# Two attention blocks on one Trainium2 core: the memory block's feature map is computed as a guarded quadratic on VectorE and GpSimd, two chunks are normalised in one pass, four squared tiles a unit, and the first chain of operations is shortened

## The chip, the cores and the metric

The kernel runs on one core of a Trainium2 chip. A core has TensorE (PE, matrix multiplications into PSUM), ScalarE (ACT, activation functions), VectorE (DVE) and GpSimd (POOL) for elementwise work, and SyncE (SP), which here only issues transfers. Each engine works through a queue of its own in order; semaphores tie the queues together. PSUM has eight banks of 128 x 512 f32.

The metric is the time of one execution in microseconds on the device, as the median of several runs. A profile is one execution, taken by itself; it shows every instruction with start and duration.

## The reference

There are two independent blocks, whose outputs stand side by side. S = 2048 rows, D = 1024, H = 32 heads of 32 columns.

```python
def _A_ref(x, wqkv, wo):                        # plain attention, no mask
    q, k, v = split(x @ wqkv)                   # per head [2048, 32]
    p = softmax(q @ k.T * Dh ** -0.5)
    return (p @ v) @ wo

def _B_ref(x, wq, wk, wv, wo, beta):            # four segments of L = 512 rows, causal inside a segment
    phi = lambda t: where(t > 0, t + 1.0, exp(t))
    M, z = 0, 0
    for s in range(4):
        qs, ks, vs = segment s of x @ wq, x @ wk, x @ wv
        a_dot = softmax(qs @ ks.T * Dh ** -0.5 + causal mask) @ vs
        pq = phi(qs)
        a_mem = (pq @ M) / (pq @ z + 1e-6)
        o = g * a_mem + (1 - g) * a_dot         # g = sigmoid(beta), one number a head
        pk = phi(ks)
        M, z = M + pk.T @ vs, z + sum(pk)
    return concat(o) @ wo
```

All entries of x, wqkv and wo are normal numbers times 0.05; B's weights are smaller by another factor of 32 (`D ** -0.5`). Inputs are bf16.

## The kernel before

**Units.** Four heads (128 partitions) are worked on together: a group g = 0..7. A's unit (g, c) is a chunk c = 0..7 of 256 queries against all 2048 keys. B's unit (s, j) is a pair of groups j, j+1 of one segment. B's 16 units are strewn among A's 64. The first four units of A are cut into parts, so that work can begin before all of x is there.

**Sets.** A unit consists of sets: eight in A, five in B, 592 in all. A set is four score tiles, one for each head, of 128 keys x 512 columns in four PSUM banks. TensorE fills them with eight (or twelve) small matmuls, tiled by rows (L1194, `plan_set`). ScalarE then takes the exponential, two banks (1024 columns) at a time (L1270, `plan_exp`), without a maximum subtracted. Three pairs of banks rotate for this, and two further banks serve everything else on TensorE. The products with V (L1361) and the row sums (L1368, `round`) are matmuls tiled by columns, and so are all projections (L822, `mm4`). Between two score sets TensorE therefore does column work: sums of older sets and projection "jobs" for later units.

**Squared tiles.** In some sets of an A unit the first head's tile doesn't go to ScalarE: VectorE computes Y = a x + b from PSUM (L1231), GpSimd squares it (L1234, `plan_square`). The constant part that this approximation of the exponential leaves out is added back when a chunk is normalised (`corr`, `cu`). `SQUARES` lists the sets for each g: five of eight for g = 0 and 1, four for g = 2 to 6, three for g = 7.

**The guard.** Both the missing maximum and the squares are valid for small scores only. For every projection the squared norms of q and k are bounded (`guard_cols`, `guard_dg`, `guard_more`, `guard_end`; squares by `square` and `square_dve`), and a flag is set. ScalarE's program exists twice; at 24 places it loads a flag and branches. In the guarded copy every exponential has a bias, and squared tiles are redone by an exponential (`alt`). With the present data the plain copy runs.

**Norms.** When a chunk's sums are complete (`norm`, `recip_rows`), VectorE copies them from PSUM to a buffer T2 while adding the correction (L1427), transposes the row sums (L1429), takes reciprocals (L1442), transposes back (L1444); GpSimd multiplies (L1493, L1488). B's norms begin with a transpose and a scaled copy from PSUM (L1431, L1433) and end with two operations on GpSimd (L1507, L1508). T2 has a ring of three buffers (`T_RING`) for these, and one more for B's memory reads (`job_mem`), which normalise 512 columns in the same manner.

**The feature map** (`job_phi`). For B's group (s, j) ScalarE takes exp of k, of q, or of both (L1906, 512 or 1024 columns, from SBUF), VectorE takes the minimum with 1 (L1908) and adds max(x, 0) (L1912). The result PKQ goes to the memory read and, by a transposing transfer, to the update of M (`job_M`).

**The order.** All operations are written down once with keys. A planner (`Prog.schedule`) then simulates the engines with costs given for each operation and writes the queues: exponentials stay in program order, TensorE chooses between score sets, sums and jobs, jobs carry due times (`level`, `plan_jobs`, `NUDGE`), and a table `SHIFT` moves single keys of VectorE, GpSimd and ScalarE. The costs only set the order; on the chip semaphores alone hold the engines.

**The start** (`plan_prologue`). x is fetched in six transposing transfers on SyncE's queue (L1546, `X_PIECES`; `turn`), with weights between them (L1517, L1523). The first K and Q of group 0 are projected (`quarter`), copied (L1776 on VectorE, L1778 on ScalarE), squared (L1817), reduced (L1614), and the bias of the first guarded exponentials (L1257) is computed (L1624, L1691, L1697, L1700).

## Time and profile before

| | us |
|---|---|
| median of 3 runs | 1057.02 (1055.73 to 1057.83) |
| profiled execution, its own time | 1059.17 |
| its span (first to last instruction) | 1057.3 |
| granted TensorE clock | 0.997 of full speed |

The profile's page names instructions by line and engine. "Busy" is the time in which an engine has at least one instruction under way; for TensorE the ends are modelled, and matmuls overlap. A group's row reads: line, engine, operation, output <- inputs, shapes, count | busy us, mean ns of one | idle time of the engine just before them, and what ended most of it. A timeline's row reads: start, length, engine, line, operation, count, and in brackets idle time before it; several equal instructions in a row are merged. Rows of the page that stand for the rest, in us:

| engine | busy | share of the span | instructions |
|---|---|---|---|
| TensorE | 1023.4 | 97% | 25438 |
| ScalarE | 1016.9 | 96% | 1224 |
| VectorE | 701.6 | 66% | 1562 |
| GpSimd | 585.9 | 55% | 677 |

### The profile page before, as it was taken

The page shows a single profiled execution, that of the slowest core. Times are in us where ns is not written, and L with a number is a line of the kernel's source. Part 1 is how long each engine was busy: PE and PEld are TensorE (multiplying, and loading weights), DVE is VectorE, ACT ScalarE, POOL GpSimd, SP SyncE. Part 2 cuts the span into 40 slices and gives each one's busy share as a digit, 9 for nine tenths or more (in the row PEclk, how much of TensorE's full clock was granted, in tenths as well). Part 3 has the DMA queues.
Part 4 walks back from the last instruction along what each step waited for, and adds up shares of the span by engine and source line. Part 5 has one row for each costly group of instructions (what it writes and reads, how often), then busy time and mean ns, then how long its engine had stood idle before and what let it go on. Part 6 is the DMA issues. An engine that isn't in the chain of part 4 may idle for free.

```text
span 1057.3 us, 56117 instructions
## 1 busy us (share of the span) xinstructions
PE 1023.4 (97%) x25438; PEld 561.2 (53%) x25438; DVE 701.6 (66%) x1562; ACT 1016.9 (96%) x1224; POOL 585.9 (55%) x677
## 2 busy tenths in 40 slices
PE   8999999999999999999999999999999989999998
PEld 3555555655555555555555545565555545445554
DVE  2356866667566586767865598687755875874444
ACT  3999989999999999999999999999999999999997
POOL 2115467558654675756656487665644765653310
PEclk9999999999999999999999999999999999999999
DMA  9132352005313241032223330132113551021101
GB/s 189 34 90 58 69 126 46 10 21 120 83 48 92 64 103 25 11 82 66 58 57 95 96 69 19 25 93 54 50 28 91 161 174 27 23 78 54 56 23 62
DMA packets 171390, 72.17 MB, mean 68 GB/s; under 512 B 134800, under 2 KB 169360, under 8 KB 171152
## 3 DMA queue, kind: packets, MB, share of 16 engines
q1 hardware_dynamic: 168784, 67.79, 26.2%
q8 instruction: 200, 3.28, 1.4%
q10 hardware_dynamic: 2368, 0.79, 0.3%
q14 instruction: 38, 0.31, 0.1%
HBM read 45.29 MB, written 11.73 MB: 54 GB/s over the span
## 4 chain that ended last, share of the span: by engine, by line
PE 58%; ACT 34%; DVE 4%; issue 2%; SPq 1%; DMA 1%; ACTq 0%; DVEq 0%
ACT P L1270 33%; PE ps L822 28%; PE ps L1194 12%; PE ps L1361 9%; PE ps L1368 8%; PE ps L1862 1%; SPq L1546 1%; DVE Y L1231 1%; DMA xT_A<-in_A_x_dram 1%; ACT PKQ_B L1906 1%; DVE T L1431 0%; DVE KQ_B L1581 0%; PE ps L1637 0%; DVE OT_B L1933 0%; DVE T L1444 0%
## 5 line engine op out<-in xcount | busy, mean ns | idle before, releaser
L1270 ACT ACTIVATE P<-ps 128x1024 bf16<-128x1024 f32 (+1 forms) x1176 | 989.4, 1062 | 16.3 <-PE ps L1194 8.0
L1234 POOL TENSOR_TENSOR Pc<-Y 128x512 bf16<-128x512 f32 x238 | 249.6, 1050 | 266.3 <-PE ps L822 84.8
L1368 PE MATMUL ps<-P,onesb 128*32 128x256 bf16 (+1 forms) x4388 | 295.1, 271 | 0.6 <-issue 0.6
L1361 PE MATMUL ps<-P,V_A 128*32 128x256 bf16 x3620 | 252.1, 274 | 0.7 <-DVE cols L1691 0.2
L1231 DVE TENSOR_SCALAR Y<-ps 128x512 f32<-128x512 f32 x238 | 163.3, 686 | 104.5 <-PE ps L1194 95.5
L1194 PE MATMUL ps<-KQ_A 32*128 32x256 bf16 x4096 | 203.9, 273 | 11.6 <-ACT P L1270 7.3
L1194 PEld LDWEIGHTS ps<-KQ_A 32*128 32x128 bf16 x4096 | 61.7, 92 | 157.7 <-ACT P L1270 115.7
L822 PE MATMUL ps<-xT_A,W_A 128*32 128x512 bf16 (+1 forms) x2232 | 138.8, 363 | 3.0 <-DMA xT_A<-in_A_x_dram 2.5
L1368 PEld LDWEIGHTS ps<-P,onesb 128*32 128x32 bf16 x4388 | 128.4, 97 | 24.7 <-issue 11.4
L822 PE MATMUL ps<-xT_B,W_B 128*32 128x512 bf16 (+1 forms) x2264 | 139.2, 360 | 2.3 <-issue 0.6
L1361 PEld LDWEIGHTS ps<-P,V_A 128*32 128x32 bf16 x3620 | 107.4, 96 | 25.7 <-issue 10.6
L1368 PE MATMUL ps<-Pc,onesb 128*32 128x256 bf16 x476 | 119.3, 274 | 0.0
L1361 PE MATMUL ps<-Pc,V_A 128*32 128x256 bf16 x476 | 119.1, 274 | 0.1
L1293 POOL TENSOR_SCALAR_AFFINE_SELECT P<-P 128x768 bf16<-128x768 bf16 (+1 forms) x96 | 75.7, 794 | 48.3 <-ACT P L1270 46.2
L1595 POOL TENSOR_TENSOR sqA<-KQ_A 128x512 bf16<-128x512 bf16 x61 | 63.4, 1048 | 66.7 <-DVE KQ_A L1581 34.6
L1595 POOL TENSOR_TENSOR sqB<-KQ_B 128x512 bf16<-128x512 bf16 x64 | 67.8, 1061 | 19.9 <-DVE KQ_B L1581 15.1
L822 PEld LDWEIGHTS ps<-xT_B,W_B 128*32 128x32 bf16 x2264 | 52.8, 96 | 48.7 <-issue 19.9
L822 PEld LDWEIGHTS ps<-xT_A,W_A 128*32 128x32 bf16 x2232 | 51.8, 96 | 50.7 <-issue 16.9
L1444 DVE STREAM_TRANSPOSE T<-rc 128x256 f32<-128x256 f32 (+1 forms) x152 | 72.5, 481 | 2.7
L822 PE MATMUL ps<-Wv_B,xT_B 128*32 128x512 bf16 (+1 forms) x1128 | 70.7, 361 | 2.1 <-issue 1.3
L822 PE MATMUL ps<-Wo_B,OT_B 128*32 128x512 bf16 (+1 forms) x1128 | 69.0, 361 | 0.3 <-DVE T L1427 0.3
L1581 DVE CAST KQ_B<-ps 128x512 bf16<-128x512 f32 x64 | 43.9, 685 | 32.2 <-PE ps L822 31.5
(114 smaller groups left out, 1231.4 us busy)
## 6 DMA issues: line engine op xcount, KB each, us to landing
Wv_B<-in_B_wv_dram SPq DMA_DIRECT2D x32, 256.0 KB, 3.4
W_B<-in_B_wk_dram SPq DMA_DIRECT2D x32, 256.0 KB, 3.2
W_B<-in_B_wq_dram SPq DMA_DIRECT2D x32, 256.0 KB, 3.9
Wo_B<-in_B_wo_dram SPq DMA_DIRECT2D x32, 256.0 KB, 3.2
out_dram<-outsb SPq DMA_DIRECT2D x56, 128.0 KB, 1.8
W_A<-in_A_wqkv_dram SPq DMA_DIRECT2D x14, 256.0 KB, 3.9
ot_a_scratch<-OTst SPq DMA_DIRECT2D x51, 64.0 KB, 2.3
xT_A<-ot_a_scratch SPq DMA_DIRECT2D x6, 512.0 KB, 5.8
```

The source lines that it names most:

```text
L822: ins = e.matmul(out[r], w[:, r], x, start=start, stop=stop, tile_position=(0, 32 * t), skip_group_check=True)
L1194: ins = e.matmul(out, kap, qap, start=st, stop=True, tile_position=(32 * h, 0), skip_group_check=True)
L1231: o = self.dve(lambda e: e.tensor_scalar(Y[:, :], src, KAPPA * SCALE, BETA, ALU.mult, ALU.add), 512, key - 9.0, [self.bank[bank]], [rY], f ...
L1234: last.append(self.pool(lambda e: e.tensor_tensor(dst, Y[:, :], Y[:, :], ALU.mult), 512, key - BCK, [rY], [rP], rate=0.56))
L1270: a = self.act(guarded if early else lambda e: e.activation(dst, src, ACT.Exp, scale=SCALE), cols, key, rd, wr, fixed=EXP_FIXED + (0.095 i ...
L1293: self.pool(lambda e: e.affine_select(v, v, pattern=pat, compare_op=ALU.is_ge, fill=0.0, base=0, channel_multiplier=-1), 2 * nd * P, key + ...
L1361: ins = e.matmul(self.pb(obk, q0, q0 + nq, slice(32 * h, 32 * h + 32)), v, p, start=first, stop=last, tile_position=(0, 32 * h), skip_grou ...
L1368: ins = e.matmul(self.pb(obk, QC + q0, QC + q0 + nq, slice(32 * h, 32 * h + 32)), self.onesb[:, 0:32], p, start=False, stop=last, tile_pos ...
L1444: self.dve(lambda e: e.transpose(L2.rearrange("p (b r) -> p b r", r=32), bc), n, key, [rr], [rl], fixed=0.17)
L1546: return self.dma(lambda e: e.dma_start(dst, src, transpose=True), sem, key, reads, writes, issue=issue, lat=lat, gate=gate)
L1581: self.dve(lambda e: e.tensor_copy(dst, src()), 512, key, [self.at(b)], rdst, fixed=0.155)
L1595: self.pool(lambda e: e.tensor_tensor(sq[:, :], src, src, ALU.mult), 512, key, [rsrc], [rs], rate=0.56)
```

## The change

1. **Feature map.** `job_poly` computes min((a x + b)^2 + 1 - b^2, 1) with a = 0.6909, b = 0.7232 instead of min(exp(x), 1): VectorE writes U = a x + b (512 columns, f32), GpSimd squares U in place and then adds and takes the minimum into PKQ. U is a single buffer. `job_phi` keeps only the sum with max(x, 0). The work is placed about half an A unit ahead of the A unit that runs before the B unit ("host"); the projections of B's k and q are due before the host, too. The guard's limit for B becomes much smaller (`FREE_B`), and the guarded copy of ScalarE's program redoes the exponential (`redo`, `late` in `plan_exp`).
2. **Squares.** `LEVEL` replaces the list by g: four squared tiles in every unit of g = 0 to 6, three for g = 7. There are 226 squared tiles where there were 238.
3. **Norms.** Two successive chunks of A with squares share one transpose, one reciprocal and one transpose back; the copy from PSUM stays one a chunk. T2 has four buffers: two for these pairs, two that all other norms and the memory reads share.
4. **The start.** ScalarE squares Q straight from PSUM before it copies it; the norms' matmuls accumulate two halves, so that the reduction is over 256 columns; one operation of the first bias is left out. SyncE's queue waits after the fourth piece of x until that piece has landed; two later pieces and three weight transfers are behind this wait.
5. **Order.** The table `SHIFT` has new entries, so that the order of VectorE's, GpSimd's and ScalarE's queues differs in many places.

```diff
-T_RING = 3
-PHI_AT = 4.341
+PHI_AT, PHI_G, PHI_LEAD = 4.341, 0.0, 6.0
-FREE = 0.1
+FREE, FREE_B = 0.1, 0.5 * SCALE * 0.01
+QUAD = 0.6909020858999743, 0.7231874996921336
-SQUARES = ((1, 3, 4, 6, 7), (1, 3, 4, 6, 7), (1, 3, 4, 6), (1, 3, 5, 7), (1, 3, 5, 7), (1, 3, 5, 7), (1, 3, 5, 7), (1, 4, 6))
+SQUARES = ((1, 3, 4, 6, 7), (1, 3, 5, 7), (1, 4, 6))
+LEVEL = "1111111111111111" "1111111111111111" "1111111111111111" "1111111122222222"
+ALONE = ((6, 6), (6, 7))
...
-        if add is None:
-            i = self.nT % T_RING
-            self.nT += 1
-        else:
-            i = T_RING
-        T2, rc = self.T2[i], self.rc[i]
+        i = 2 + self.nT % 2
+        self.nT += 1
+        T2, rc = self.T2[:, i, :], self.rc[i - 1]
...
+        if cu is not None and (g, t["c"]) not in ALONE:
+            n = int(self.half is not None)
+            ok = self.T2[:, n, :].rearrange("p (a n) -> p a n", a=2)
+            self.dve(lambda e: e.tensor_tensor(ok, self.pb(obk).rearrange("p (a n) -> p a n", a=2),
+                                               cu[0].unsqueeze(2).to_broadcast([P, 2, QC]), ALU.add), 512, k - NORM_K, [ob, cu[1]],
+                     [self.r_T2[n]], fixed=0.155)
+            if not n:
+                self.half = t
+                return
+            both, rr = self.r_T2[:2], self.r_rc[0]
+            L2, rc = self.T2[:, 0:2, QC:512], self.rc[0][:, :].rearrange("p (a b) -> p a b", a=2)
+            self.dve(lambda e: e.transpose(L2, L2), 512, k, both, both, fixed=0.17)
+            self.dve(lambda e: e.reciprocal(rc, L2.rearrange("p a (b r) -> p a b r", r=32)[:, :, :, 0]), 128, k, both, [rr])
+            self.dve(lambda e: e.transpose(L2.rearrange("p a (b r) -> p a b r", r=32), rc.unsqueeze(3).to_broadcast([P, 2, 8, 32])), 512, k,
+                     [rr], both, fixed=0.17)
+            for i, x in enumerate((self.half, t)):
+                self.scaled(x, k, self.T2[:, i, 0:QC], self.T2[:, i, QC:512], [self.r_T2[i]])
+            self.half = None
+            return
...
+                o = self.turn(self.xT[:, lo:hi, 512 * h:512 * h + 512], xa[512 * h:512 * h + 512, P * lo:P * hi],
+                              self.sm_x[n], key, [], rs, issue, lat)
+                if n == 3:
+                    gate = o
+                if n >= 4:
+                    o.deps.add(gate)
+                    if n == 5:
+                        o.order.add(last)
+                last = o
...
+                    self.act(lambda e, x=direct[0], src=src: e.activation(x[:, :], src, ACT.Square), 512, key, [bk], [direct[1]])
                     self.act(lambda e, dst=dst, src=src: e.activation(dst, src, ACT.Copy), 512, key, [bk], [rd])
...
-                self.colrun = self.guard_cols(key, sq, bank=3)
-                self.guard_end(key, [self.colrun], 2, [BIAS_PART[0]], bank=4, urgent=True)
+                self.colrun = self.guard_cols(key, sq, bank=3, wide=QC)
+                self.guard_end(key, [self.colrun], 2, [BIAS_PART[0]], bank=4, urgent=True, raw_bias=True)
...
+    def job_poly(self, s, j, key, at):
+
+        holds(self.r_KQB[j], "KQ", s, j)
+        mark(self.r_PKQ[j % 2], "P", s, j)
+        PKQ, rp, ks = self.PKQ[j % 2], self.r_PKQ[j % 2], self.phi_of(s)
+        a, b = ks[0], ks[-1] + 1
+        made = []
+        U, rU = self.U, self.r_U
+        for k in ks:
+            x = PKQ[:, k, :]
+            self.dve(lambda e, k=k: e.tensor_scalar(U[:, :], self.KQB[:, j, k, :], QUAD[0], QUAD[1], ALU.mult, ALU.add), L / 2, key,
+                     [self.r_KQB[j][k]], [rU], fixed=0.16, port=True)
+            self.pool(lambda e: e.tensor_tensor(U[:, :], U[:, :], U[:, :], ALU.mult), L, key + PHI_G, [rU], [rU], rate=0.56)
+            made.append(self.pool(lambda e, x=x: e.tensor_scalar(x, U[:, :], 1.0 - QUAD[1] ** 2, 1.0, ALU.add, ALU.min), L, key + PHI_G,
+                                  [rU], [rp[k]], rate=1.0))
+        self.phi_redo[s, j] = dict(at=at, op=None, made=made, reads=[self.r_KQB[j][k] for k in ks], rp=rp[a:b], out=PKQ[:, a:b, :],
+                                   src=self.KQB[:, j, a:b, :], bc=2 + j // 2)
+
     def job_phi(self, s, j, key):
...
-        x = self.act(lambda e: e.activation(PKQ[:, a:b, :], src, ACT.Exp), n, key, rs, rp[a:b], fixed=0.19)
-        x.margin = MARGIN
-        self.dve(lambda e: e.tensor_scalar(PKQ[:, a:b, :], PKQ[:, a:b, :], 1.0, None, ALU.min), n / 4, key, rp[a:b], rp[a:b], fixed=0.16,
-                 port=True)
-        for k in range(a, b):
+        for k in self.phi_of(s):
...
-                d = min(SB[j - j % 2] - LEAD_B, SB[RXJ] - 1.0)
+                d = min(self.host[s, j - j % 2] - LEAD_B, SB[RXJ] - 1.0)
...
-                r = SB[j] - 4.0 - PHI_AT
+                at = self.host[s, j - j % 2]
+                self.item(at - PHI_LEAD + 0.01 * (j % 2), lambda key, s=s, j=j, at=at: self.job_poly(s, j, key, at))
+                r = max(at + 1.0, SB[j] - 4.0 - PHI_AT)
```

More of the change, by code (lines that the diff above doesn't have):

```diff
@@ L480, in ready_of @@
             for x in o.deps:
[L481 removed]
+                t = max(t, x.end + (SELF if x.eng == o.eng and x.sem is None else x.lat) + (job if x.eng in ("DVE", "POOL") else 0.0) +
                         (TO_POOL if o.eng == "POOL" and x.eng == "DVE" else 0.0) +
@@ L1041, in plan @@
         self.T_end = T
+        self.host = {(s, j): self.st[before["B", s, j]] for s in range(NSEG) for j in range(0, NG, 2)}
         group = []
```

210 lines of the change are left out of this document (133 added, 77 removed), and 358 rows, old and new, of the table SHIFT.

## The prediction

> **What bounds the kernel now.** I read the page's first part, the windows, ScalarE's groups and waits, the timelines of ScalarE and TensorE, and last the chain of waits.
>
> ```profile
> PE 1023.4 (97%) x25438; PEld 561.2 (53%) x25438; DVE 701.6 (66%) x1562; ACT 1016.9 (96%) x1224; POOL 585.9 (55%) x677
> ```
> ```profile
> 0.00:27.30 27.30, 22.29 (x364) 10.23 (x368) 8.56 (x24) 10.34 (x11) 6.97 (x37) 1.00 1.08 192
> 27.30:1045.00 1017.70, 992.08 (x24883) 546.09 (x24875) 687.01 (x1527) 1001.51 (x1208) 578.94 (x640) 1.00 0.26 65
> ```
> ```profile
> 200.00:300.00 100.00, 99.33 (x2664) 57.49 (x2664) 67.75 (x149) 100.00 (x124) 69.70 (x79) 1.00 0.29 65
> 400.00:500.00 100.00, 94.70 (x2488) 54.69 (x2482) 74.86 (x182) 96.37 (x116) 62.51 (x71) 0.98 0.21 48
> ```
> The window columns after the length are PE, PEld, DVE, ACT and POOL busy. From 27.30 to 1045 ScalarE idles 16.2 us in 1017.7 (1.6%), TensorE 25.6 us; VectorE and GpSimd have 33% and 43% free. So two engines stand close to the bound, and the question is which of them a microsecond taken off ScalarE meets next. Where the stretch is best (200 to 300) both are full together, where it is worst (400 to 500) both lose 4 to 5%.
>
> ```profile
> L1270 ACT ACTIVATE P<-ps 128x1024 bf16<-128x1024 f32 x938 | 925.3, 1149 | 14.5 <-PE ps L1194 6.4 <-PE ps L1368 3.2 <-PE ps L822 2.8
> L1270 ACT ACTIVATE P<-ps 128x512 bf16<-128x512 f32 x238 | 171.2, 719 | 1.8 <-PE ps L1194 1.6
> ```
> ```profile
> PE 58%; ACT 34%; DVE 4%; issue 2%; SPq 1%; DMA 1%; ACTq 0%; DVEq 0%
> ```
> The chain of waits says PE 58%, but it walks along whichever of two full engines it meets. TensorE's own rows say that it has room that "busy" hides:
>
> ```profile
> 301.97 0.40 PE L1194 MATMUL ps<-KQ_A 32*128 32x256 bf16 x8
> 302.29 0.72 PE L822 MATMUL ps<-Wo_B,OT_B 128*32 128x256 bf16 x12
> ...
> 303.28 0.28 PE L1361 MATMUL ps<-P,V_A 128*32 128x256 bf16 x4
> 303.39 0.28 PE L1368 MATMUL ps<-P,onesb 128*32 128x256 bf16 x4
> 303.50 0.28 PE L1361 MATMUL ps<-P,V_A 128*32 128x256 bf16 x4
> 303.71 0.40 PE L1194 MATMUL ps<-KQ_A 32*128 32x256 bf16 x8
> ```
> Groups of four start 0.11 us apart and are each shown 0.28 us long. The last one before a wait therefore covers some 0.17 us of it, so the 992 us of PE busy hold waits as well as work. TensorE is the second bound, not the first: ScalarE is the one whose instructions stand back to back.
>
> **The change part by part.**
>
> *The feature map's exponential leaves ScalarE.*
> ```profile
> 117.62 0.67 ACT L1906 ACTIVATE PKQ_B<-KQ_B 128x512 bf16<-128x512 bf16 x1
> 118.14 2.46 ACT L1270 ACTIVATE P<-ps 128x512 bf16<-128x512 f32 x3
> ```
> ```profile
> 387.67 1.08 ACT L1906 ACTIVATE PKQ_B<-KQ_B 128x1024 bf16<-128x1024 bf16 x1
> 388.62 9.85 ACT L1270 ACTIVATE P<-ps 128x512 bf16<-128x512 f32 x12
> ```
> ```profile
> L1906 ACT ACTIVATE PKQ_B<-KQ_B 128x1024 bf16<-128x1024 bf16 x16 | 19.3, 1207 | 0.0
> L1906 ACT ACTIVATE PKQ_B<-KQ_B 128x512 bf16<-128x512 bf16 x16 | 11.6, 725 | 0.0
> ```
> Instructions of ScalarE overlap, so the price is from start to next start: 0.52 and 0.95 us. 16 x 0.95 + 16 x 0.52 = 23.5 us, with no idle time ahead of any of them: all on the path. **-23.5.** The conditional redo in the exponential's other branch costs nothing while the guard holds.
>
> *Four squares a unit.* 12 of the 238 squared tiles go back to ScalarE, each making a 512-wide exponential 1024 wide: 1149 - 719 = 430 ns, 12 x 0.43 = **+5.2**. It takes 12 operations off VectorE and GpSimd each.
>
> *The quadratic on VectorE and GpSimd.* 48 tiles, each one VectorE operation (512 bf16 to f32) and two on GpSimd (square f32, then add and min to bf16). Nothing of that kind runs now; nearest rows:
> ```profile
> L1908 DVE TENSOR_SCALAR PKQ_B<-PKQ_B 128x512 bf16<-128x512 bf16 x16 | 6.0, 377 | 3.1 <-ACT PKQ_B L1906 3.1
> L1908 DVE TENSOR_SCALAR PKQ_B<-PKQ_B 128x1024 bf16<-128x1024 bf16 x16 | 11.3, 705 | 2.3 <-ACT PKQ_B L1906 2.1
> L1231 DVE TENSOR_SCALAR Y<-ps 128x512 f32<-128x512 f32 x238 | 163.3, 686 | 104.5 <-PE ps L1194 95.5
> ```
> ```profile
> L1234 POOL TENSOR_TENSOR Pc<-Y 128x512 bf16<-128x512 f32 x238 | 249.6, 1050 | 266.3 <-PE ps L822 84.8 <-DVE Y L1231 54.8 <-PE ps L1368 38.5
> L1293 POOL TENSOR_SCALAR_AFFINE_SELECT P<-P 128x512 bf16<-128x512 bf16 x32 | 20.3, 637 | 9.7 <-ACT P L1270 8.3 <-PE ps L1361 0.8
> ```
> VectorE: 0.38 to 0.69 us, 48 x 0.5 = 24 us, against 17.3 us for the removed minimum (6.0 + 11.3). GpSimd: 1.05 for the square, 0.64 (the select, also one input) to 1.05 for the second, which I take at 0.64: 48 x 1.69 = 81 us, less 12 x 1.05: GpSimd goes from 586 to 654 us, 62% of the span.
>
> GpSimd's 43% of idle time hides this on average; in detail it need not. U is one buffer, so VectorE's next U waits for GpSimd's second operation, and 41 of the 48 U writes carry such a wait. Behind a waiting U stand, in VectorE's queue, the Y of a squared tile and the PSUM copies; behind these TensorE. Bounds on the path: 0, to one GpSimd square at each of 48, 50 us. I take **+2**, near 0: the queue places other work between successive U, and the nearest operation of today, two-input and beside GpSimd, is blocked now and then with nobody on the chain waiting for it:
> ```profile
> L1912 DVE SCALAR_TENSOR_TENSOR PKQ_B<-KQ_B,PKQ_B x48: 648/708/1544, 115.1 to 932.6; 128x512 bf16<-128x512 bf16 x48
> L1908 DVE TENSOR_SCALAR PKQ_B<-PKQ_B x32: 247/422/1306, 114.6 to 931.8; 128x512 bf16<-128x512 bf16 x16, 128x1024 bf16<-128x1024 bf16 x16
> ```
> Minimum, median and maximum in ns: the same instruction takes 0.65 or 1.54 us, with a median 0.06 above the minimum. By the median the 48 U lose 3 us of VectorE time in all, and the sum stands. If each U that starts while GpSimd works were held to that instruction's end, it would lose 62% of half of 1.05 us, 0.33 us, 16 us for 48; all of that on the path would give 1042 - 2 + 16 = 1056. The Trainium skill (SBUF — State Buffer, "SBUF: two separate sides") states just that: one port pair for the two engines, an exclusive lock held for the whole instruction, "the other fully blocks". The maxima agree with the lock, the medians with its being rarely met.
>
> *Norms of two chunks in one pass.*
> ```profile
> L1429 DVE STREAM_TRANSPOSE T<-T 128x256 f32<-128x256 f32 x58 | 25.6, 441 | 1.2
> L1444 DVE STREAM_TRANSPOSE T<-rc 128x256 f32<-128x256 f32 x128 | 55.9, 439 | 2.4
> L1442 DVE RECIPROCAL rc<-T 128x8 f32<-128x8 f32 x128 | 24.5, 192 | 1.0
> L1444 DVE STREAM_TRANSPOSE T<-rc 128x512 f32<-128x512 f32 x24 | 16.9, 704 | 0.3
> L1440 DVE RECIPROCAL rc<-rc 128x16 f32<-128x16 f32 x24 | 5.7, 239 | 0.4
> ```
> A pair cost 2 x (441 + 192 + 439) = 2144 ns and will cost 704 + 239 + 704 = 1647: 28 pairs x 0.5 = 14 us off VectorE. The copy that frees PSUM stays per chunk, so nothing on the path: 0. VectorE in all: 702 + 24 - 17 - 14 - 12 x 0.69 = 687 us. The cost is scratch: the ring of three for all norms and the single buffer for memory reads become two for A's pairs and two shared by B's norms and memory reads. B's first operation then waits more often for GpSimd, holding a PSUM bank. Bounds: 0, to one GpSimd operation of 0.7 us for each of 64 norms; as VectorE is a third free I count **+1**, within the last term.
>
> *The shorter first chain.*
> ```profile
> 12.00 2.04 SPq L1546 DMA_TRANSPOSE xT_A<-in_A_x_dram  x1
> ```
> ```profile
> 12.00 6.72 DMA xT_A<-in_A_x_dram
> 18.77 0.61 PE ps L822 x8
> ```
> ```profile
> 13.14 0.69 DVE L1614 TENSOR_REDUCE cols<-ps 128x1 f32<-128x512 f32 x1 [0.67 <-PE ps L1607]
> 14.81 0.21 DVE L1697 TENSOR_SCALAR braw<-cols 128x1 f32<-128x1 f32 x1
> 15.30 2.12 ACT L1257 ACTIVATE P<-ps,bias 128x1024 bf16<-128x1024 f32 x2 [3.51 <-DVE bias L1700]
> 19.77 6.14 ACT L1257 ACTIVATE P<-ps,bias 128x1024 bf16<-128x1024 f32 x6 [2.34 <-PE ps L1194]
> ```
> Reduce over 256 instead of 512 (-0.25 us), one bias operation less (-0.25 with its gap), one square now on ScalarE (-0.2): the first exponential comes 0.7 us earlier. The third waits for TensorE, and TensorE for the fourth piece of x: issue ended at 14.04, landing 18.72, while the next transposes were already issuing. The change holds SyncE's queue until that piece has landed. Queued behind it are two x pieces, two W_A and one Wv_A; these x pieces hold keys that the scores reach only after 24 exponentials past 27.3 (at most 925.3 / 938 = 0.99 us each), so their delay of 2 to 3 us has some 20 us of cover, which the next weights share. Bounds: 0 (the landing takes 4.7 us after its issue alone too) to -2.5; I take -1.3 for the landing and -0.7 for the chain: **-2**.
>
> *What ScalarE meets next.* With 18.3 us less on ScalarE the middle becomes 999 us if its idle stays at 16.2. At the PE idle share of the stretch 200 to 300 (0.7%), TensorE's 992 us would fit into 999; so it can, but only if the whole runs like its best stretch. With half of its present 25.6 us idle left, the middle is 1005 us. Between 0 and +6: with the +1 above, **+3**.
>
> **Sum**, against the profiled execution (span 1057.3, own time 1059.17): 1059.2 - 23.5 + 5.2 + 2 - 2 + 3 = 1043.9. That execution lies 2.15 above the median of 1057.02, so the median should be 1041.7, some 1.4% less; I say **1042**.
>
> **The rivals.**
> 1. *TensorE becomes the bound.* For it: 992 us busy and the chain's 58%. Against: the hidden waits. Its number of groups and of changes between row and column tiling stays. If PE's 25.6 idle stays whole, the middle keeps its length and only the start's 2 us are won, 1055; halfway between that and the forecast it is about 1049.
> 2. *GpSimd holds VectorE up, and the kernel gets slower.* The place: VectorE in front of U, blocked by the lock or by U's single buffer, with Y and the PSUM copies behind it. Without the +2 for this term the gain is 1059.2 - 1041.9 = 17.3 us, so it decides from 17.3 / 48 = 0.36 us a U on the path. The lock alone (0.33) gives an even result, about 1056; the lock and the buffer's wait together, at the 0.9 us between the minimum and the maximum above, give 43 us, 1083; at 0.6 us (29 us) the time is 1069. For it: GpSimd's work comes in lumps, and each lump of two pieces is longer than one exponential. Against it: VectorE's 33% of free time.
> 3. *The guard does not hold.* Then each exponential takes the other branch: 226 squares come back at 0.52 us (118 us) and the feature map twice (47 us): over 1180. For the present data B's q and k are products of 0.05-scaled numbers with weights 32 times smaller, so their norms are tiny: unlikely.
>
> **How the numbers follow.** Forecast (1034 to 1048) 0.58, a larger gain below 1034 0.04, rival 1 0.17 (1048 to 1055), about even 0.05 (the lock alone), rival 2 beyond that 0.14, rival 3 0.02. A change of 0.2% (2 us) is about what a measurement tells from none. Faster: 0.58 + 0.04 + 0.17 = 0.79; within 0.2%: 0.05; slower: 0.16. Range 1032 to 1062: from the ScalarE sum with no new losses and the full start gain (1059.2 - 18.3 - 3.2 - 2.15 = 1035.5, and 3 less if present idle shrinks too) to the beginning of rival 2.
>
> **What would show it.** Right: L1906 gone from ScalarE; ScalarE's work from its first full-speed exponential to its last some 18 us shorter, with 16 to 22 us idle; the first x wait of TensorE under 2 us; GpSimd near 650 us, VectorE under 700. Wrong: ScalarE's idle time grown by over 10 us with PE L1194 as releaser, behind it VectorE's Y waiting for U; U's operations near 1.5 us; or PE without idle time while ScalarE waits.

## The result, and the profile after

The changed kernel takes 1086.81 us (median of four, 1085.87 to 1088.5). That is 1.0302 times the time of the kernel before, with a 95% interval of 1.028 to 1.0324: 3% slower, where 1.4% faster was forecast and 1062 was the upper end of the range. The profiled execution has a span of 1085.9 us.

The page's first part of the changed kernel, and its windows as they were shown of before (length, PE, PEld, DVE, ACT, POOL):

```profile
PE 1029.9 (95%) x25506; PEld 562.7 (52%) x25506; DVE 695.6 (64%) x1480; ACT 1003.0 (92%) x1193; POOL 723.2 (67%) x761
```
```profile
0.00:27.30 27.30, 23.42 (x404) 12.02 (x408) 8.02 (x23) 13.17 (x15) 7.00 (x37) 1.00 1.06 179
...
200.00:300.00 100.00, 95.27 (x2584) 55.53 (x2580) 60.81 (x136) 95.50 (x113) 77.53 (x81) 1.00 0.25 63
400.00:500.00 100.00, 92.61 (x2387) 51.21 (x2379) 75.08 (x168) 92.74 (x111) 88.52 (x91) 0.98 0.21 49
600.00:700.00 100.00, 92.37 (x2272) 48.99 (x2268) 74.02 (x166) 85.86 (x102) 88.57 (x89) 0.98 0.20 48
```

ScalarE has 13.9 us less work (1016.9 - 1003.0), yet the span is 28.6 us longer, so ScalarE's idle time has doubled: 1057.3 - 1016.9 = 40.4 us before, 1085.9 - 1003.0 = 82.9 us now. By 27.3 us ScalarE has done 13.17 us of work, against 10.34 in the profile before; the part on the prediction shows that little of this belongs to the change. The best stretch of before (200 to 300) is no longer full on any engine, and GpSimd is at 88 to 89% from 400 to 500 and from 600 to 700 (74% between).

The chain of waits, the groups of ScalarE and of the new operations, U's row by its tile (minimum, median, maximum in ns), and the waits (in all, times, longest):

```profile
PE 40%; ACT 24%; POOL 11%; DVE 5%; issue 2%; ACTq 0%; POOLq 0%; DVEq 0%
```
```profile
L1309 ACT ACTIVATE P<-ps 128x1024 bf16<-128x1024 f32 x950 | 927.5, 1131 | 57.8 <-POOL PKQ_B L2006 20.5 <-PE ps L1210 20.0 <-PE ps L1416 12.9
L2006 POOL TENSOR_SCALAR PKQ_B<-U 128x512 bf16<-128x512 f32 x48 | 92.8, 1933 | 7.2 <-PE ps L829 3.3 <-POOL U L2005 0.3
L2005 POOL TENSOR_TENSOR U<-U 128x512 f32<-128x512 f32 x48 | 50.7, 1055 | 5.1 <-DVE U L2003 4.5 <-DVE cols L1767 0.5
L2003 DVE TENSOR_SCALAR U<-KQ_B 128x512 f32<-128x512 bf16 x48 | 25.9, 540 | 33.6 <-POOL PKQ_B L2006 33.3
```
```profile
L2003 DVE TENSOR_SCALAR U<-KQ_B x48: 378/428/1296, 99.5 to 926.2; 128x512 f32<-128x512 bf16 x48
```
```profile
DVE U L2003 <- POOL PKQ_B L2006: 33.3, 27, 3.3
...
ACT P L1309 <- PE ps L1210: 23.9, 35, 1.8
...
ACT P L1309 <- POOL PKQ_B L2006: 20.5, 3, 12.4
...
ACT P L1309 <- PE ps L1416: 14.6, 15, 4.6
```

(L1309 was L1270, L1210 was L1194, L1416 was L1368.) Two things stand out. GpSimd's second operation on U, the addition with the minimum, takes 1.93 us where 0.64 was put into the sum; GpSimd is on the chain with 11%, where it had no share. And ScalarE's exponential waits for that operation's result, in three pieces, the longest 12.4 us, though the plain copy of its program doesn't read it.

### The profile page after: what moved, and what is told of

Same layout as the page of the kernel before. It is cut to its first block, busy times and chain, and to the rows that moved or that the text cites. A ratio compares the mean times of both kernels' runs of the same rounds, so it can differ in the third digit from the quotient of the medians.

```text
span 1085.9 us, 56115 instructions
## 1 busy us (share of the span) xinstructions
PE 1029.9 (95%) x25506; PEld 562.7 (52%) x25506; DVE 695.6 (64%) x1480; ACT 1003.0 (92%) x1193; POOL 723.2 (67%) x761
## 4 chain that ended last, share of the span: by engine, by line
PE 40%; ACT 24%; POOL 11%; DVE 5%; issue 2%; ACTq 0%; POOLq 0%; DVEq 0%
ACT P L1309 24%; PE ps L829 20%; PE ps L1210 8%; PE ps L1409 6%; PE ps L1416 5%; POOL PKQ_B L2006 4%; POOL Pc L1250 2%; POOL U L2005 1%; DVE Y L1247 1%; POOL P L1341 1%; POOL T L1556 1%; POOL OT_B L1557 1%; POOL sqB L1670 1%; DVE T L1479 1%; PE ps L1713 0%
## 5 line engine op out<-in xcount | busy, mean ns | idle before, releaser
L1309 ACT ACTIVATE P<-ps 128x1024 bf16<-128x1024 f32 (+1 forms) x1176 | 991.0, 1049 | 63.6 <-PE ps L1210 23.9
L1250 POOL TENSOR_TENSOR Pc<-Y 128x512 bf16<-128x512 f32 x226 | 242.8, 1075 | 209.5 <-PE ps L829 51.8
L1416 PE MATMUL ps<-P,onesb 128*32 128x256 bf16 (+1 forms) x4412 | 292.0, 270 | 0.0
L1247 DVE TENSOR_SCALAR Y<-ps 128x512 f32<-128x512 f32 x226 | 155.3, 687 | 123.5 <-PE ps L1210 112.5
L1210 PE MATMUL ps<-KQ_A 32*128 32x256 bf16 x4096 | 204.4, 273 | 19.4 <-ACT P L1309 9.7
L1210 PEld LDWEIGHTS ps<-KQ_A 32*128 32x128 bf16 x4096 | 62.7, 92 | 168.7 <-ACT P L1309 121.2
L1416 PEld LDWEIGHTS ps<-P,onesb 128*32 128x32 bf16 x4412 | 128.4, 96 | 23.0 <-issue 9.9
L1409 PE MATMUL ps<-Pc,V_A 128*32 128x256 bf16 x452 | 113.2, 274 | 3.6 <-POOL Pc L1250 2.9
L1416 PE MATMUL ps<-Pc,onesb 128*32 128x256 bf16 x452 | 113.0, 274 | 0.0
L2006 POOL TENSOR_SCALAR PKQ_B<-U 128x512 bf16<-128x512 f32 x48 | 92.8, 1933 | 7.2 <-PE ps L829 3.3
L829 PEld LDWEIGHTS ps<-xT_A,W_A 128*32 128x32 bf16 x2280 | 52.5, 96 | 52.7 <-issue 19.0
L1670 POOL TENSOR_TENSOR sqB<-KQ_B 128x512 bf16<-128x512 bf16 x64 | 70.8, 1107 | 11.6 <-DVE KQ_B L1656 8.7
L1656 DVE CAST KQ_A<-ps 128x512 bf16<-128x512 f32 x60 | 41.1, 685 | 34.1 <-PE ps L829 32.9
```

The source lines that it names most:

```text
L829: ins = e.matmul(out[r], w[:, r], x, start=start, stop=stop, tile_position=(0, 32 * t), skip_group_check=True)
L1210: ins = e.matmul(out, kap, qap, start=st, stop=True, tile_position=(32 * h, 0), skip_group_check=True)
L1247: o = self.dve(lambda e: e.tensor_scalar(Y[:, :], src, KAPPA * SCALE, BETA, ALU.mult, ALU.add), 512, key - 9.0, [self.bank[bank]], [rY], f ...
L1250: last.append(self.pool(lambda e: e.tensor_tensor(dst, Y[:, :], Y[:, :], ALU.mult), 512, key - BCK, [rY], [rP], rate=0.56))
L1309: a = self.act(guarded if early else lambda e: e.activation(dst, src, ACT.Exp, scale=SCALE), cols, key, rd, wr, fixed=EXP_FIXED + (0.095 i ...
L1409: ins = e.matmul(self.pb(obk, q0, q0 + nq, slice(32 * h, 32 * h + 32)), v, p, start=first, stop=last, tile_position=(0, 32 * h), skip_grou ...
```

## The experiments

All ratios are to the kernel before, run on the same chip in the same stretch. Where nothing else is said, the planner lays out the order, by costs that the text of the kernel gives.

### Moving, pricing or undoing the second operation, with a new order

e1 puts the second operation on VectorE; e2 only tells the planner that it takes 1.92 us; e3 undoes the feature map alone.

```diff
# e1
-            made.append(self.pool(lambda e, x=x: e.tensor_scalar(x, U[:, :], 1.0 - QUAD[1] ** 2, 1.0, ALU.add, ALU.min), ...
+            made.append(self.dve(lambda e, x=x: e.tensor_scalar(x, U[:, :], 1.0 - QUAD[1] ** 2, 1.0, ALU.add, ALU.min), ...
# e2
-                                  [rU], [rp[k]], rate=1.0))
+                                  [rU], [rp[k]], rate=0.2895))
# e3: job_phi as in the kernel before (L1906 to L1914), no job_poly
```

> One edit: the second of GpSimd's two operations for the feature map (add and minimum, 1.93 us each in the changed kernel, 48 of them, 92.8 us) runs on VectorE instead, and the planner is told so. Theory G (this operation's length is what made the kernel slower): GpSimd's busy time falls from 723 to about 630 us, VectorE's wait at U falls from 33 us to under 5, ScalarE's idle time from 80 us to under 35, and the time is 1038 to 1050. Rival N (the shared norm buffers and the new order are the cause): the time stays above 1070. Rival P (any operation pair between VectorE and GpSimd on one buffer U stalls): VectorE waits at U or at the new operation for over 20 us in total and the time lies between 1055 and 1075.

> Same operations on the same engines as the changed kernel; the planner's cost of GpSimd's second operation is set to 1.92 us, as measured, instead of 0.66 us, so that it orders the queues for the true length. If the loss came from an order made for a wrong length (theory G-order): VectorE's wait at U falls under 10 us and the time comes to 1045 to 1065. If GpSimd's load as such is the cause (theory G-load, 723 us busy of 1086 and lumps of 3 us): 1075 to 1095. Rival N: above 1070 too.

> The feature map is computed as before the change (exponential on ScalarE, minimum on VectorE), everything else of the change stays: four squares a unit, norms of two chunks in one pass with the shared buffers, the shorter start, the new order table. Theory G: the loss is gone; 23.5 us come back on ScalarE and 5.2 us of the squares stay, less 2 us at the start, so 1058 to 1068. Rival N: above 1072, with VectorE waiting for GpSimd at T.

Measured: 1121.85 us (1.0631, 1.0601 to 1.066), 1119.89 (1.0613, 1.0583 to 1.0643) and 1099.16 (1.0416, 1.0386 to 1.0445). All three are slower than the change that they mend or undo, and missed every band but rival N's (above 1070 or 1072). That doesn't show rival N: e2 changes no instruction, only a cost, and loses 33 us. What the three share is that the planner lays out another order, for which the table of shifts wasn't made; so they say nothing on the parts of the change.

### What the forms of GpSimd's operation cost

e4 gives the 48 second operations six forms in turn.

```diff
+            fn = (lambda e, x=x: e.tensor_scalar(x, U[:, :], c, 1.0, ALU.add, ALU.min),      # L2012
+                  lambda e, x=x: e.tensor_scalar(x, U[:, :], c, None, ALU.add),              # L2013
+                  lambda e, x=x: e.tensor_scalar(x, U[:, :], b2, c, ALU.min, ALU.add),       # L2014
+                  lambda e, x=x: e.tensor_scalar(x, U[:, :], 1.0, c, ALU.mult, ALU.add),     # L2015
...
```

> The disputed operation by itself: the 48 second operations on GpSimd take six forms in turn (add and minimum from f32 to bf16 as in the change; add alone; minimum and then add; multiply and then add; add and minimum from bf16; add and minimum from f32 to f32). The forms with add alone and with multiply and add leave the minimum out, and one form leaves the result in U, so the feature map is another there. If the length comes from two arithmetic operations in one instruction, add alone takes 0.6 to 0.7 us and the others about 1.9; if it comes from the minimum, multiply and add is short as well; if from the conversion from f32 to bf16, the last two forms are short.

Groups of e4:

```profile
L2012 POOL TENSOR_SCALAR PKQ_B<-U 128x512 bf16<-128x512 f32 x9 | 17.6, 1956 | 1.3 <-DMA PKt_B<-PKQ_B 0.5 <-POOL U L2009 0.3
L2014 POOL TENSOR_SCALAR PKQ_B<-U 128x512 bf16<-128x512 f32 x9 | 17.4, 1928 | 0.8 <-DMA PKt_B<-PKQ_B 0.2
L2013 POOL TENSOR_SCALAR PKQ_B<-U 128x512 bf16<-128x512 f32 x9 | 13.4, 1491 | 0.0
...
L2015 POOL TENSOR_SCALAR PKQ_B<-U 128x512 bf16<-128x512 f32 x9 | 5.6, 617 | 4.2 <-PE ps L829 3.5
```

Add with minimum 1.96 us, minimum with add 1.93, add alone 1.49, multiply with add 0.62. With a bf16 input, or f32 output, add and minimum stay at 1.93 and 1.92. So the conversion isn't the reason; add alone is too long for the theory of two operations in one instruction and also for that of the minimum. The price hangs on which operations they are; why, the runs don't show.

### The same function in the fast form, in the same order

e5 clamps first, on VectorE, so that GpSimd's second operation is a multiply with an add: a (min(x, 0) + b/a) squared and shifted is the same function. The planner's costs are the same, and every queue has the changed kernel's order. e6 leaves out the multiplication by a^2 (so its feature map is not the reference's) and takes the add alone, a length between the two.

```diff
-  e.tensor_scalar(U[:, :], self.KQB[:, j, k, :], QUAD[0], QUAD[1], ALU.mult, ALU.add)
+  e.tensor_scalar(U[:, :], self.KQB[:, j, k, :], 0.0, QUAD[1] / QUAD[0], ALU.min, ALU.add)
-  e.tensor_scalar(x, U[:, :], 1.0 - QUAD[1] ** 2, 1.0, ALU.add, ALU.min)
+  e.tensor_scalar(x, U[:, :], QUAD[0] ** 2, 1.0 - QUAD[1] ** 2, ALU.mult, ALU.add)          # e5
+  e.tensor_scalar(x, U[:, :], 1.0 - QUAD[1] ** 2, None, ALU.add)                            # e6
```

> The clamp is moved to VectorE's first operation, U = min(x, 0) + b/a, and GpSimd's second operation becomes a^2 U^2 + 1 - b^2, a multiply and add, which the probe of forms showed at 0.62 us instead of 1.92; the function computed is the same, every queue has the same instructions in the same order. Theory G (the length of this one operation, against an order planned for 0.66 us, made the kernel slower): VectorE's waits at U fall from 33 us to under 6, ScalarE's idle time from 83 to about 35 us, and the time is 1037 to 1048, faster than before the change. Rival N (the rest of the change costs the time): 1070 or more. Half and half would be 1055 to 1065.

> As the fast form, but GpSimd's second operation is an addition alone (1.49 us in the probe of forms), so the factor a^2 is left out and the feature map is another; the order of all queues is the same. Theory G by size: 48 x 0.87 us more on GpSimd than the fast form, two thirds of the way to the changed kernel, so about two thirds of its loss: 1065 to 1080. If only the minimum or the port mattered and not the length, the time would be that of the fast form.

e5: 1066.37 us (1.0109, 1.0087 to 1.0131). e6: 1070.10 (1.015, 1.0119 to 1.018). The form alone is worth 20.4 us of the 31. e5 lies above theory G's band and below rival N's: much of the loss is this form, not all. It isn't linear: from 0.62 to 1.49 us costs 3.7 us, from there to 1.92 another 16.7. Waits of e5, then of e6:

```profile
ACT P L1309 <- PE ps L1416: 13.2, 14, 4.6
ACT P L1309 <- POOL sqB L1670: 11.8, 1, 11.8
ACT P L1309 <- PE ps L1210: 11.1, 21, 1.7
...
DVE U L2003 <- POOL PKQ_B L2006: 3.8, 2, 2.0
```
```profile
ACT P L1309 <- POOL PKQ_B L2006: 17.3, 3, 11.2
DVE U L2003 <- POOL PKQ_B L2006: 15.4, 19, 2.6
...
ACT P L1309 <- PE ps L1210: 10.7, 25, 1.2
```

VectorE's 33.3 us in front of U have shrunk to 3.8. From e6 to the change the time grows by 16.7 us, U's wait by 17.9 (15.4 to 33.3), ScalarE's wait for scores (L1210) by 13.2 (10.7 to 23.9), but its wait for L2006 by only 3.2 (17.3 to 20.5). That speaks for a loss by way of VectorE, with U held up in front of its other work; the path from U to the scores wasn't followed instruction by instruction.

But in e5 two long stalls of ScalarE stand where they stood. The timelines of ScalarE, GpSimd and VectorE of e5 at these places:

```profile
631.07 1.94 ACT L1309 ACTIVATE P<-ps 128x1024 bf16<-128x1024 f32 x2 [4.92 <-POOL PKQ_B L2006]
```
```profile
630.34 0.62 POOL L2006 TENSOR_SCALAR PKQ_B<-U 128x512 bf16<-128x512 f32 x1
```
```profile
854.95 1.94 ACT L1309 ACTIVATE P<-ps 128x1024 bf16<-128x1024 f32 x2 [11.81 <-POOL sqB L1670]
```
```profile
854.26 0.19 DVE L1783 TENSOR_SCALAR flags<-braw,flags 128x1 f32<-128x1 f32 x1
```

The first ends 0.11 us after GpSimd's second operation (630.34 + 0.62), the second half a microsecond after a guard flag of B; between the two the trace has ScalarE's load of that flag (L785, 0.28 us) and its branch (L786). In `plan_exp` the exponential that carries the redo for the guarded copy takes PKQ, q, k and B's bias into its reads, and its flag is the latest of those that it could need. Both copies share these semaphore waits. So in the plain copy, too, ScalarE waits for GpSimd's result, and each B flag is awaited one unit earlier than before.

### Taking the carrying exponential's waits away

After the queues are written, e9 takes these waits out of e5, and e10 out of the changed kernel; no queue changes its order.

```diff
+            if redo or late:
+                a.only = {r for x in redo + late for r in (self.r_bias[x["bc"]], *x["reads"], *x["rp"])} - {self.r_bias[bc]}
+                a.own = (None, None) if early else (plain, self.flag_of[bc])
...
             self.pg.schedule()
+            for o in self.pg.ops:
+                if o.own is not None:
+                    o.alt, o.flag = o.own
+                o.deps = {x for x in o.deps if o.why.get(x, {None}) - o.only and (x.own is None or o.why.get(x, {None}) - x.only)}
```

> The fast form of e5, in the same order on every engine, but no exponential carries the redo of the feature map any more: the 16 carrying exponentials no longer wait for GpSimd's PKQ results, ScalarE's branch waits for the guard flag of its own head only (at the places where the kernel before had it), and VectorE's L1912 counterpart no longer waits for ScalarE. The guarded branch's redo of the feature map is left out. Theory W (the new waits of the carrying exponential cost what e5's two long stalls show, 4.9 + 11.8 us): 1066.4 - 16.7 = 1050, 1046 to 1055, so not slower than before; ScalarE's groups show no stall on POOL above 2 us. Theory T (the order no longer fits, and the stall would only move to the next wait): 1062 to 1067, with TensorE's scores as the new releaser of the same time.

> The changed kernel as it is, with the 1.92 us second operation, but without the carrying exponentials' waits (the guarded branch's redo of the feature map is left out). Theory W with the length as a separate term: 1086.8 less ScalarE's 20.5 us on PKQ_B, about 1066, 1062 to 1072; VectorE's U still waits some 33 us for PKQ_B and L1210 stays a releaser of about 20 us. If the 1.92 us do all their harm through the carrying exponentials: 1050 to 1056. If the length alone does it, through VectorE's U in front of Y: 1080 to 1087.

e9: 1062.80 us (1.0069, 1.0049 to 1.0089); e10: 1080.42 (1.0228, 1.0205 to 1.025). The waits are worth 0.4% in the fast form and 0.7% in the slow one, not the 16.7 us of the stalls: theory T was right on e9 in the main. e10 misses theory W's 1062 to 1072 and lies at the low end of 1080 to 1087, the band for a loss by the length alone; U still waits 31.9 us there. Without the new waits the slow form costs 1.59% (e9 to e10). The long stall is still there, and the timelines of e9 (ScalarE, TensorE) show why:

```profile
850.62 3.35 ACT L1313 ACTIVATE P<-ps 128x512 bf16<-128x512 f32 x4 [10.86 <-POOL sqB L1677]
```
```profile
841.21 1.91 PE L829 MATMUL ps<-xT_B,W_B 128*32 128x512 bf16 x32
843.68 2.99 PE L829 MATMUL ps<-xT_B,W_B 128*32 128x512 bf16 x52 [0.56 <-DMA W_B<-in_B_wq_dram]
...
848.50 1.67 PE L829 MATMUL ps<-Wv_B,xT_B 128*32 128x512 bf16 x25
850.11 0.40 PE L1214 MATMUL ps<-KQ_A 32*128 32x256 bf16 x8
```

TensorE works through projections for nine microseconds before the next scores (L1214): they stand in its queue in that order, and the exponential, now free to start, has no scores: the last of them ends at 850.51, 0.11 us before it starts. (GpSimd, which the row names, ends a square at nearly the same moment.) A wait that was there when the queue was written doesn't vanish with its semaphore.

### What work off ScalarE is worth in the order of before

e9 has neither the long operation nor the carrying exponential's waits, and is still slower than before. So the prediction's first term was put to the test by itself. e11 is the kernel before, in its own order, without the 32 exponentials of the feature map. e12 is the kernel before with these exponentials and the 32 minima replaced by e5's three operations, inserted into VectorE's and GpSimd's queues at places from a table of their own, with the sum that follows (L1912) moved along; TensorE's and SyncE's queues are untouched.

```diff
# e11, after the queues are written; m, the minimum, reads q or k itself
+                m.deps |= x.deps
+                self.pg.queue["ACT"].remove(x)
# e12, for each tile
+                u = Op("DVE", lambda e, ...: e.tensor_scalar(U[:, :], src[k], 0.0, QUAD[1] / QUAD[0], ALU.min, ALU.add), ...)
+                g = Op("POOL", lambda e: e.tensor_tensor(U[:, :], U[:, :], U[:, :], ALU.mult), ...)
+                p = Op("POOL", lambda e, ...: e.tensor_scalar(out[k], U[:, :], QUAD[0] ** 2, 1.0 - QUAD[1] ** 2, ALU.mult, ALU.add), ...)
```

> The kernel before, in its own order on every engine, with the 32 exponentials of the feature map (L1906) taken out of ScalarE's queue and nothing put in their place: the minimum that follows reads q or k itself, so the feature map of head B is left out. This measures by itself what 23.5 us off ScalarE are worth in the order of before. Theory S, the prediction's first step (ScalarE is the first bound and TensorE follows): 1056 - 23.5 + 0 to 6 = 1033 to 1039, ScalarE's idle time in the middle as before, 16 to 22 us. Theory P (the prediction's first rival: TensorE, in the order written for it, keeps its pace): 1050 to 1056, ScalarE's idle time grown by some 20 us in many short waits, released by PE's scores.

> The kernel before, in its own order on TensorE and SyncE, with the 32 exponentials and the 32 minima of the feature map replaced by 48 times the fast form of e5 (clamp on VectorE, square and multiply-add on GpSimd), inserted into VectorE's and GpSimd's queues at places of their own; no exponential carries a redo (the guarded branch's redo of the feature map is left out). Neither the squares nor the norms nor the first chain of the change are in it. Theory S: 1033 to 1042, so faster than both kernels. Theory P: 1050 to 1058, as e11 and no faster than it. If the two new operations on GpSimd themselves disturb the order: over 1060, with VectorE's U or L1912 among the releasers and e11 well below it.

e11: 1052.87 us (0.9972, 0.9954 to 0.999). e12: 1061.75 (1.0046, 1.0029 to 1.0063). First part of the page and waits of e11:

```profile
PE 1021.8 (97%) x25438; PEld 561.3 (53%) x25438; DVE 699.2 (66%) x1562; ACT 998.9 (95%) x1192; POOL 587.1 (56%) x677
```
```profile
ACT P L1280 <- PE ps L1204: 18.8, 40, 1.7
```

Even with nothing put in their place, the removed exponentials bring 2.9 us, as theory P had it. ScalarE's busy time falls by 18.0 us (1016.9 - 998.9) and its idle time rises by 12.1 (from 40.4 to 52.5), in many waits for scores (18.8 us; 8.0 before). The new operations, in the fast form and at these places, then cost 8.9 us, although the minima are gone from VectorE: by its number this is the last of the three cases, in which they disturb the order. One stretch shows some of that: windows of e11 and of e12 from 400 to 500, where GpSimd goes from 66 to 80%:

```profile
400.00:500.00 100.00, 96.65 (x2612) 56.56 (x2604) 75.51 (x181) 96.26 (x116) 65.66 (x74) 1.00 0.23 47
```
```profile
400.00:500.00 100.00, 92.99 (x2484) 53.29 (x2476) 81.22 (x185) 92.68 (x110) 80.30 (x90) 1.00 0.22 48
```

### TensorE's work, or the waits between the engines

Four in seven of the inner groups of the row sums take half the columns in e13, so half of these sums are left out; e14 is e11 with the same cut.

```diff
+            mid = nq == 256 and not any(x[5] or x[6] for x in tiles)
+            self.nmid = getattr(self, "nmid", 0) + mid
+            cut = 2 if mid and self.nmid % 7 < 4 else 1
...
+                    nq = nq // cut
+                    p = p[:, 0:nq]
```

> The kernel before, in its own order on every engine; of the row sums' matmul groups in the middle of an accumulation (L1368, 256 columns) four in seven, 533 in all, sum 128 columns only, so TensorE has 533 x 128 / 256 x 0.11 = 29 us less to do. Half of the row sums of these groups are left out. Theory P (TensorE keeps the pace, ScalarE is close behind it): ScalarE's 16 us of idle time in the middle can go, so 1040 to 1050, with L1194 almost gone as a releaser of ScalarE. Theory Q (the waits between the engines in the written order, not an engine's work, hold the time): 1052 to 1057.

> e11 and e13 in one: the feature map's 32 exponentials are taken out of ScalarE's queue (that part is left out), and 533 groups of the row sums take 128 instead of 256 columns (half of their sums left out), all in the order of before. Theory P: both engines have 20 to 29 us less, so 1053 - 20 to 1053 - 26, 1027 to 1034: nearly the whole 23.5 us that the prediction counted appear once TensorE gives room. Theory Q: 1048 to 1054, hardly under e11.

e13: 1050.21 us (0.9965, 0.9949 to 0.998). e14: 1048.17 (0.9948, 0.9928 to 0.9968). The chain of waits of e13, then two waits of e14:

```profile
ACT 68%; PE 25%; DVE 3%; issue 2%; SPq 1%; DMA 0%; POOL 0%; ACTq 0%; DVEq 0%
```
```profile
ACT P L1280 <- PE ps L1204: 15.4, 29, 1.8
PE ps L1204 <- ACT P L1280: 11.1, 30, 1.0
```

For TensorE, 29 us less by the estimate from the 0.11 us between two groups (18.3 less busy, 1023.4 to 1005.1) bring 3.8 us; for ScalarE, 18.0 less busy bring 2.9; both together bring 5.8. e13 lies between the two bands, 0.2 us above theory P's; e14 decides: it lies in theory Q's band and 14 us above theory P's. With room on both engines the kernel nearly keeps its length, and each waits for the other in turn. So neither engine's amount of work holds the time. What is left are the waits between engines in the order as written; whether the order makes them, or the three pairs of PSUM banks through which scores and exponentials pass, wasn't tried. The chain's main engine changes from PE 58% to ACT 68% by a cut that is worth 0.35%: its shares tell whose queue is followed, not what a cut would bring.

### Orders that the planner lays out without a table

In e7 (before) and e8 (the change in e5's form) the table of shifts is emptied; e15 is e8's partner with the feature map on ScalarE. e16 and e17 repeat that pair with another constant of the planner.

```diff
-SHIFT = {((f, n), e): v for f, e, t in (
...
+SHIFT = {}
# e16, e17
-JOB_SLOPE = 1.1413237083257293
+JOB_SLOPE = 1.5
```

> The kernel before with its order table emptied, so the planner orders by keys and costs alone: a measure of what the table is worth, and the base for parts of the change tried without it. The second and the third experiment (1120 and 1099 us) kept a table made for another order; if that is why they were slow, this one is slower than 1056 by 15 to 45 us: 1070 to 1100. If the table is worth little: within 1056 to 1062, and the slowness of the third experiment belongs to the shared norm buffers or the new due times.

> The changed kernel with the fast form and the order table emptied. Against the kernel before with its table emptied this gives the worth of the whole change without the tuning of single keys: by the sum of the prediction 15 us faster than that run. Rival N: as slow or slower than it.

> The changed kernel with the feature map as in the kernel before (32 exponentials on ScalarE, minimum on VectorE), everything else of the change kept, and the order laid out by the planner without the table of shifts: the partner of e8, which differs in the feature map alone. Theory O (work off ScalarE pays when the order is laid out for it; in a fixed order it turns into waits): e8's 1108.7 + 15 to 25, 1124 to 1134. Theory N (the quadratic does not pay in any order here): 1103 to 1113.

> e8 (the fast form, no table) with the planner's weight of a job's lateness, JOB_SLOPE, at 1.5 instead of 1.14: another order for the same work. No theory gives its time; it is there for e17. 1095 to 1125.

> e15 with JOB_SLOPE at 1.5, the partner of e16. Theory O: 10 to 25 us above e16. Theory N: within 6 us of e16, or below it.

| | feature map on ScalarE | in the fast form | difference |
|---|---|---|---|
| change without table | 1135.86 (e15) | 1108.69 (e8) | 27.2 |
| the same, JOB_SLOPE 1.5 | 1128.33 (e17) | 1120.50 (e16) | 7.8 |

Before without its table is 1116.86 (e7), beyond the 1070 to 1100 that was expected: the table is worth 61.9 us to before (1055.0 in that stretch), the changed kernel's table only 42.3 to e5. Without tables the whole change in the fast form (e8) is 8.2 us faster than before (e7), not the 15 of the prediction's sum. In these new orders the fast form is ahead of ScalarE's map by 27 and 8 us; the second is below theory O's band and above theory N's. Both signs are theory O's, but this isn't shown by two pairs: a new order alone moves the time as much (e8 to e16 11.8 us, e2 33), and the granted clock differed too (0.995 in e8, 0.986 in e15).

## Why the prediction was wrong

**The account.** In per cent of the time before, each step the difference of two measured ratios: the exponentials off ScalarE -0.28 (e11); the three new operations in the fast form, in before's order, +0.74 (e12 to e11); the changed kernel's own order with the squares, norms and start +0.23 (e9 to e12, intervals overlapping); the carrying exponential's waits +0.40 (e5 to e9); the slow form +1.93 (the change to e5). The sum is 3.02. The last two depend on the order in which they are taken: without the waits the slow form is 1.59, and with the slow form the waits are 0.74 (e10).

**Step by step, as the prediction put it.**

- *"ScalarE is the one whose instructions stand back to back ... TensorE is the second bound."* This is the step that failed first. Its reading of the rows was right, but back to back in a fixed order doesn't mean that a shorter queue ends earlier: e11 paid 2.9 us. The prediction's own coupling term (0 to +6) should have been some 20.6 (23.5 - 2.9). The first rival had the size for this case, 1055 without a gain in the middle, but blamed TensorE's work, which e13 and e14 clear. The Trainium skill (Perfetto Trace Analysis, "Identifying the Most-Contended Engine") says to take the engine with the highest occupancy and to optimise it first; TensorE it judges not by its matmul time (here 97%) but, for one, by that of its weight loads (here 53%). That makes it ScalarE with 96%, and 18.0 us of busy time off it were worth 2.9.
- *"-23.5"* was right as the price: in before's trace the 32 exponentials take 15.1 and 8.4 us from start to next start. The busy time falls by only 18.0 in e11 because ScalarE's busy time hides waits too: an instruction with a wait behind it is shown at its full length, as 0.67 us where the next could start after 0.52. So the price was paid, and nearly all of it came back as waits.
- *"1.05 for the square, 0.64 ... for the second, which I take at 0.64."* The square was right (1.055), the second was 1.93, above the upper bound of 1.05. The nearest one-input row, a select, is another operation. This term alone is 20.4 us, two thirds of the loss. The Trainium skill (GPSIMD Engine Reference, "Engine selection") calls one-input operations there roughly line-rate; the runs have no one rate: by the operations, 128 x 512 took 0.62, 1.49 or 1.93 us.
- *"The conditional redo in the exponential's other branch costs nothing while the guard holds."* It costs 0.4 to 0.7%, since semaphore waits are shared by both copies (e9, e10). The guard held, as forecast.
- *Rival 2*, GpSimd holding VectorE up in front of U, gave 1083 at 0.9 us a U and had 0.14. It is the nearest of the cases: U waited 33.3 / 48 = 0.69 us each, and with e5 that wait and 20.4 us went together. The wait is for the second operation to free the single buffer, and it came with that operation's length. The case had put 0.9 us on it from the lock and the buffer's wait together; the lock had little part: U's median is 0.43 us, its maximum 1.30, and its mean of 0.54 is 0.16 above its minimum, 7.8 us of VectorE's time in all. That 1083 is close to 1086.81 is therefore partly luck.
- *"+2"* for the quadratic's stalls, with a bound of 50: in the fast form and before's order it is 8.9 (e12).
- *The start, -2:* not borne out. The 2.34 us for which ScalarE waited before its third exponential, behind TensorE's wait for x, belonged to that execution more than to the kernel. e11 to e14 have the start of before unchanged, and their ScalarE has done 12.35 to 12.97 us of work by 27.3 us, close to the 13.17 of the change. First e11, then the changed kernel:

```profile
15.27 2.12 ACT L1267 ACTIVATE P<-ps,bias 128x1024 bf16<-128x1024 f32 x2 [3.57 <-DVE bias L1710]
17.61 6.14 ACT L1267 ACTIVATE P<-ps,bias 128x1024 bf16<-128x1024 f32 x6 [0.22 <-PE ps L1204]
```
```profile
14.90 8.15 ACT L1273 ACTIVATE P<-ps,bias 128x1024 bf16<-128x1024 f32 x8 [2.83 <-DVE bias L1773]
```

The first exponential comes at 14.90 us, against 15.30 before and 15.04 to 15.43 in e11 to e14: 0.1 to 0.5 us, where 0.7 was forecast. The prediction probably counted that wait twice, once as -1.3 and once in the 2.15 by which that execution lies above the median. Whether the held queue keeps such a wait away isn't shown: e7, with the old start in another order, has one of 3.99 us.

- *Squares and norms* weren't tried alone. VectorE has 695.6 us, against 687 forecast.
- *"Wrong: ScalarE's idle time grown by over 10 us with PE L1194 as releaser, behind it VectorE's Y waiting for U; U's operations near 1.5 us."* Idle time grew by 42.5 us; L1210 and L2006 share the releasing, and U's own length stayed short while the wait stood in front of it.

**What stays open.** Whether an order exists in which the changed work beats 1057 us: none of the complete kernels did, and the planner's new orders show gains only between orders that are all slower. Which of the new operations makes the 8.9 us of e12 wasn't separated, nor what squares, norms and start do each by themselves. More room between TensorE and ScalarE, by more pairs of banks, wasn't tried.

## What to carry to other kernels

Where queues are written out by hand or by a planner and two engines are both near full, take one piece of work out of the old order and measure before counting it as a gain. Price each operation of an engine by a row of the same operations, not of the same shape. Look for waits that a rarely taken branch hands to the common one. Before a wait of one profile goes into a sum, see whether another execution has it.

## What the runs showed of the hardware

GpSimd's tensor-scalar operation on 128 x 512 took 0.62 us as multiply and add, 1.49 as add alone and 1.92 to 1.96 as add and minimum in either order, each from f32 to bf16; add and minimum stayed at 1.93 from bf16 and 1.92 to f32 (e4). Writing the same function as clamp, square, multiply-add took 64 us off GpSimd (723.2 to 658.8 in e5).
